# Top-32 attention with a gated feed-forward: weighted values of a head pair formed once per row group, and a longer lag from row 1920 on

## The chip, the cores and the metric

The kernel runs on one core of a Trainium2 chip. The metric is the time of one execution on the device in microseconds (us). TensorE is called PE here, its weight loads PEld, VectorE DVE, ScalarE ACT, GpSimd POOL and SyncE SP; SP issues all DMAs.

## The reference

Eight batches of eight heads attend over 576 rows with 64 channels a head. Of each row's 576 scores the 32 largest are kept, the softmax runs over these, and the result multiplies the values. The rows of all batches (8 x 576 = 4608, 512 channels each) then go through a gated feed-forward.

```python
scores = scale * np.matmul(q, k.transpose(0, 1, 3, 2))
kth = np.partition(scores, -top_k, axis=-1)[..., -top_k:-top_k + 1]
scores = np.where(scores >= kth, scores, -1000000000.0)
attn = np.exp(scores - np.max(scores, axis=-1, keepdims=True))
attn = attn / (np.sum(attn, axis=-1, keepdims=True) + 1e-09)
x = np.matmul(attn, v)             # then (4608, 512)
gate = 1.0 / (1.0 + np.exp(-(x @ w_gate)))
return gate * (x @ w_val) @ w_out  # d_ff = 1536
```

## The kernel before

**Tiling.** Attention works on one head pair of one row tile at a time (a step): 128 rows, or 64 for the fifth tile of a batch. Even batches are cut into the row groups tiles 0 to 2 and 3 to 4, odd ones into tiles 0 to 1 and 2 to 4; `steps` runs over row groups, then over the four head pairs, then over the tiles of the group. The feed-forward works on twelve units of 384 rows (`U`); a unit becomes available when the last row group that it needs is through for all four pairs.

**A step.** `scores` (L186) multiplies on PE and copies the scores from PSUM on ACT. `select` (L254) finds the 32nd largest with DVE, ACT and POOL, `masked` (L222) keeps what lies above it and forms in `inv` (L230) the reciprocal of the row sums. `turn` (L303) transposes the weights on PE into PSUM tiles `pt` (pool `ps_t`, two buffers), which ACT copies to the tile `et` (two buffers).

**The weighted values.** `weigh` (L322) is called for every two row tiles or for the rest of a group: 256, 128 or 64 columns. In blocks of 256 and 128 columns eight matmuls with 64-column weights (L330, L331) go in pairs, one head into the upper and one into the lower half of the PSUM tile `po` (pool `ps_o`, one buffer), and one matmul with 128-column weights (L332, `mixed`, the key chunk that both heads share) ends the sum. In the 64-column block there are eight with 64-column weights (L335, L336) and two with 64x64 weights (L337, L338). Each matmul on these plain f32 operands stands twice in the trace. Then `inv` is transposed into the same PSUM tile (L341), ACT copies it to `rs` (L344), DVE multiplies (L347 or L351), and ACT and POOL form the high and the low part of x (`xh`, `xl`; L354, L355).

**Order.** One program order is written out by `run`: attention steps, with the feed-forward's generators drawn in between. Through the first twenty-odd steps `split_weights` also splits the weights in high and low parts; when it is done, the pools `x` and `spare` are opened (`"spare" in pools`). From then on the feed-forward is drawn until its work reaches `goal = at - LAG`, where `at` is the number of attended rows and `LAG` is 448. A scheduler with its own timeline then sorts the instructions of each engine by priority, so matmuls of different parts come to stand between one another; each engine runs its own list strictly in that order.

The stretch of PE that the prediction speaks of is the whole list from about 250 us on. These lines decide when `weigh` is called:

```python
            if len(invs) == 2 or i >= end - 1 or i == NT - 1:
                ...
                weigh(et, values[g, p], o, invs, pieces, nm)
```

Of the kernel before, what the change touches and what calls it, by code (L numbers as in the profile page):

```python
# [10 lines left out]
F32 = mybir.dt.float32  # L11
# [5 lines left out]
AF = mybir.ActivationFunctionType  # L17
ALU = mybir.AluOpType
# [11 lines left out]
def tile_topk_attention_then_gated_ffn(  # L30
# [8 lines left out]
    nc = tc.nc  # L39
    P = 128  # L40
    B, H, _, S = k.shape
    D = P // 2
# [3 lines left out]
    REM = S - NT * P  # L46
# [9 lines left out]
    U = 3 * P  # L56
# [5 lines left out]
    FETCH, ASK, AHEAD = 2, 4, 2  # L62

    SOON, RUSH = 14, 22
    HELD = 2 * FG
    LAG = U + P // 2

    const = ctx.enter_context(tc.tile_pool(name="const", bufs=1))
    bi = ctx.enter_context(tc.tile_pool(name="bi", bufs=3))
# [3 lines left out]
    b1 = ctx.enter_context(tc.tile_pool(name="b1", bufs=1))  # L73
# [8 lines left out]
    ps_t = ctx.enter_context(tc.tile_pool(name="ps_t", bufs=2, space=bass.MemoryType.PSUM))  # L82
    ps_o = ctx.enter_context(tc.tile_pool(name="ps_o", bufs=1, space=bass.MemoryType.PSUM))
    ps_f = ctx.enter_context(tc.tile_pool(name="ps_f", bufs=3, space=bass.MemoryType.PSUM))

    ident = const.tile([P, P], F32, tag="ident", name="ident")
# [15 lines left out]
    pools, fresh, copies, ahead = {}, {}, [], []  # L102
# [119 lines left out]
    def masked(J, s, kth, st, e, nm):  # L222

        for j in range(J):
            nc.vector.scalar_tensor_tensor(  # L225
                e[:, j], s[:, j], kth[j], e[:, j], op0=ALU.is_ge, op1=ALU.mult, accum_out=st[:, 4 + j : 5 + j]
            )
        nc.gpsimd.tensor_scalar(st[:, 4 : 4 + J], st[:, 4 : 4 + J], 1e-9, None, op0=ALU.add)
        nc.vector.reciprocal(st[:, 6 : 6 + J], st[:, 4 : 4 + J])
        inv = bi.tile([P, P], F32, tag="inv", name=f"inv_{nm}")  # L230
        nc.gpsimd.tensor_copy(
            inv.rearrange("p (j d) -> p j d", j=J), st[:, 6 : 6 + J].unsqueeze(2).to_broadcast([P, J, P // J])
        )
        return e, inv
# [84 lines left out]
            nc.tensor.transpose(pt[:REM, 0], ef[:, NT * P : S], ident)  # L319
            nc.scalar.activation(et[:REM, 4, :P], pt[:REM, 0], AF.Copy)  # L320

    def weigh(et, vt, n, invs, pieces, nm):  # L322

        both = ps_o.tile([P, 4 * P], F32, tag="o", name=f"po_{nm}")
        po, rb = both[:, :n], both[:, 2 * P :]
        if n > REM:
            mixed = vt[:, 4:6].rearrange("p a d -> p (a d)")

            for c in reversed(range(4)):
                nc.tensor.matmul(po[D:], vt[:, 6 + c], et[:, 5 + c, :n], start=c == 3, stop=False)  # L330
                nc.tensor.matmul(po[:D], vt[:, c], et[:, c, :n], start=c == 3, stop=False)  # L331
            nc.tensor.matmul(po, mixed, et[:, 4, :n], start=False, stop=True)  # L332
        else:
            for c in range(4):
                nc.tensor.matmul(po[:D], vt[:, c], et[:, c, :REM], start=c == 0, stop=False)  # L335
                nc.tensor.matmul(po[D:], vt[:, 6 + c], et[:, c, REM:P], start=c == 0, stop=False)  # L336
            nc.tensor.matmul(po[:D], vt[:REM, 4], et[:REM, 4, :REM], start=False, stop=True)  # L337
            nc.tensor.matmul(po[D:], vt[:REM, 10], et[:REM, 4, REM:P], start=False, stop=True)  # L338

        for t, inv in enumerate(invs):  # L340
            nc.tensor.transpose(rb[:, t * P : (t + 1) * P], inv, ident)  # L341
        rs = b1.tile([P, 2 * P], F32, tag="rs", name=f"rs_{nm}")
        m = len(invs) * P
        nc.scalar.activation(rs[:, :m], rb[:, :m], AF.Copy)  # L344
        xf = rs[:, :n]
        if n > REM:
            nc.vector.tensor_tensor(xf, po, rs[:, :n], op=ALU.mult)  # L347
        else:
            for h in range(2):
                d = slice(h * D, h * D + D)  # L350
                nc.vector.tensor_tensor(xf[d], po[d], rs[d, h * REM : h * REM + REM], op=ALU.mult)  # L351
        o = 0
        for (xh, xl), c, k in pieces:
            nc.scalar.activation(xh[:, c : c + k], xf[:, o : o + k], AF.Copy)  # L354
            nc.gpsimd.tensor_tensor(xl[:, c : c + k], xf[:, o : o + k], xh[:, c : c + k], op=ALU.subtract)  # L355
            o += k
# [56 lines left out]
    def run(general):  # L413
        steps = [(g, p, i) for g, (_, first, end) in enumerate(groups) for p in range(NP) for i in range(first, end)]
        keys, values, qs, staged, xs = {}, {}, {}, {}, {}
# [34 lines left out]
            ffn_pools()  # L450
            splits = split_weights()
        todo, work, at, col, ready = [], 0, 0, 0, 0
        parts, done = {}, {}
        taken, steps_of = 0, ([2] * FG + [2, 0] * (NE // 2)) * NG

        for n in range(len(steps) + 2):
            if n < len(steps):
                g, p, i = steps[n]
                b, first, end = groups[g]
                m = n  # L460
                further = 1 if "spare" in pools else 0
                for m in range(fetched, n + FETCH + further + 1):
                    fetch(m)
                fetched = n + FETCH + further + 1
                get_values(n)
                for m in range(asked, n + ASK + further + 1):
                    ask(m)
                asked = n + ASK + further + 1
                for m in range(begun, n + AHEAD + further + 1):
                    begin(m)  # L470
                begun = n + AHEAD + further + 1
                J = 2 if i < NT else 1
                nm = f"{mark}{b}_{i}_{p}"
                if general:
                    parts[n] = select_any(J, staged.pop(n), nm)
                else:
                    parts[n] = select(J, staged.pop(n), col, nm)
                next(parts[n])
                col += J
            if n - 1 in parts:  # L480
                done[n - 1] = next(parts.pop(n - 1))
            if splits is not None:
                due = HELD * min(n + 1, SOON) // SOON
                if todo:
                    due = HELD + (2 * n_w - HELD) * (n + 1 - SOON) // (RUSH + 1 - SOON)
                while split < min(due, 2 * n_w):
                    while todo and taken < len(steps_of) and sum(steps_of[: taken + 1]) <= split:
                        work += next(todo[0])
                        taken += 1
                    next(splits)  # L490
                    split += 1
                if split == 2 * n_w:
                    while taken < len(steps_of):
                        work += next(todo[0])
                        taken += 1
                    next(splits, None)
                    splits = None
            else:
                goal = at - LAG
                goal *= 3 * (2 * NF * NP + NE * NF)  # L500
                while todo and work < goal:
                    cost = next(todo[0], None)
                    if cost is None:
                        todo.pop(0)
                    else:
                        work += cost
            if n < 2:
                continue
            g, p, i = steps[n - 2]
            b, first, end = groups[g]  # L510
            nm = f"{mark}{b}_{i}_{p}"
            e, inv = done.pop(n - 2)
            if i == first or (i - first) % 2 == 0 or i == NT:
                et, o, invs = b2.tile([P, 9, 2 * P], F32, tag="et", name=f"et_{nm}"), 0, []
            turn(e, i, et, o, nm)
            invs.append(inv)
            o += P if i < NT else REM
            if len(invs) == 2 or i >= end - 1 or i == NT - 1:

                t, left, pieces = b * S + (i + 1 - len(invs)) * P, o, []  # L520
                while left:
                    u = max(x for x, (t0, _) in enumerate(units) if t0 <= t)
                    c = t - units[u][0]
                    if (u, p) not in xs:
                        pool = bx if u % 3 < 2 else pools["x"]
                        xs[u, p] = [pool.tile([P, U], F32R, tag=x, name=f"{x}{mark}_{u}_{p}") for x in ("xh", "xl")]
                    cols = min(left, units[u][1] - c)
                    pieces.append((xs[u, p], c, cols))
                    t, left = t + cols, left - cols
                weigh(et, values[g, p], o, invs, pieces, nm)  # L530
            at += (P if i < NT else REM) / NP
            if p == NP - 1 and i == end - 1:
                while ready < len(units) and sum(units[ready]) <= b * S + min(end * P, S):
                    todo.append(ffn(f"{mark}{ready}", [xs[ready, d] for d in range(NP)], *units[ready]))
                    ready += 1
        for rest in todo:
            for _ in rest:
                pass

    run(False)  # L540


# [66 lines left out]
```

## Time and profile before

| what | value |
|---|---|
| median of the runs | 1595.59 us (1593.63, 1595.59, 1596.2) |
| the profiled execution, its own time | 1597.9 us |
| its span | 1596.1 us |
| PE busy, PEld busy | 96%, 88% |
| DVE, ACT, POOL busy | 82%, 72%, 67% |
| granted clock, mean | 0.979 of full speed |

A busy PE is not PE at its peak, since matmuls overlap: what one costs is read from the distance between the starts of two that follow each other, not from its duration. The span is cut by stretch in the windows, and the idle time of PE by its cause in the waits.

### The profile page before, as it was taken

The page shows a single profiled execution, that of the slowest core. Times are in us where ns is not written, and L with a number is a line of the kernel's source. Part 1 is how long each engine was busy: PE and PEld are TensorE (multiplying, and loading weights), DVE is VectorE, ACT ScalarE, POOL GpSimd, SP SyncE. Part 2 cuts the span into 40 slices and gives each one's busy share as a digit, 9 for nine tenths or more (in the row PEclk, how much of TensorE's full clock was granted, in tenths as well). Part 3 has the DMA queues.
Part 4 walks back from the last instruction along what each step waited for, and adds up shares of the span by engine and source line. Part 5 has one row for each costly group of instructions (what it writes and reads, how often), then busy time and mean ns, then how long its engine had stood idle before and what let it go on. Part 6 is the DMA issues. An engine that isn't in the chain of part 4 may idle for free.

```text
span 1596.1 us, 33487 instructions
## 1 busy us (share of the span) xinstructions
PE 1533.7 (96%) x10226; PEld 1403.4 (88%) x10226; DVE 1302.6 (82%) x5845; ACT 1144.5 (72%) x2547; POOL 1073.6 (67%) x1788
## 2 busy tenths in 40 slices
PE   5777999999999999999999999999999999999998
PEld 3555888789999999999999999999999999999998
DVE  7898899898988898888888889887988888877201
ACT  7788899887777777777777767767777777766221
POOL 6579765598767876777666976777667876665111
PEclk8678999999999999999999999999999999999999
DMA  7502576855555665565555665566555665564574
GB/s 241 177 27 79 180 234 234 281 185 204 190 201 209 208 235 191 205 236 204 190 201 199 223 234 190 208 225 214 191 201 199 219 220 193 192 207 168 180 283 160
DMA packets 87454, 319.99 MB, mean 200 GB/s; under 512 B 9696, under 2 KB 36320, under 8 KB 61920
## 3 DMA queue, kind: packets, MB, share of 16 engines
q1 hardware_dynamic: 87264, 317.76, 57.8%
q8 instruction: 83, 1.36, 0.3%
q14 instruction: 107, 0.88, 0.2%
HBM read 289.41 MB, written 28.31 MB: 199 GB/s over the span
## 4 chain that ended last, share of the span: by engine, by line
PE 84%; DVE 6%; ACT 4%; POOL 3%; DMA 2%; issue 2%; SPq 0%; ACTq 0%; POOLq 0%; DVEq 0%
PE pz L384 12%; PE pz L385 12%; PE pz L383 12%; PE pss L205 9%; PE pt L311 7%; PE po L330 6%; PE po L403 6%; PE po L402 6%; PE po L404 6%; PE po L332 2%; POOL u L289 2%; DMA wraw<-in_w_dram 1%; DVE cand L271 1%; PE po L341 1%; PE po L335 1%
## 5 line engine op out<-in xcount | busy, mean ns | idle before, releaser
L289 POOL TENSOR_TENSOR u<-s,under 128x288 f32<-128x288 f32 x576 | 449.1, 802 | 152.5 <-ACT under L283 143.3
L271 DVE MAX8 cand<-s 128x8 f32<-128x72 f32 x2304 | 348.2, 218 | 65.4 <-ACT s L212 63.5
L383 PE MATMUL pz<-xh,w 128*128 128x384 f32 x1056 | 362.0, 344 | 1.8 <-ACT gf L388 1.8
L384 PE MATMUL pz<-xl,w 128*128 128x384 f32 x1056 | 357.8, 339 | 0.0
L385 PE MATMUL pz<-xh,w 128*128 128x384 f32 x1056 | 357.5, 339 | 0.0
L225 DVE SCALAR_TENSOR_TENSOR e<-s,kths,e 128x576 f32<-128x576 f32 x288 | 269.6, 942 | 11.9 <-ACT e L220 10.1
L283 ACT ACTIVATE under<-s,leads 128x576 bf16<-128x576 f32 x288 | 222.6, 773 | 68.8 <-DVE leads L275 39.4
L299 DVE MAX8 kths<-u 128x8 f32<-128x584 f32 x288 | 218.7, 759 | 29.6 <-POOL u L290 28.2
L391 POOL TENSOR_TENSOR gl<-gf,gh 128x384 fp32r<-128x384 f32 x144 | 152.1, 1057 | 113.9 <-ACT gh L390 110.8
L205 PE MATMUL pss<-k,qh 128*128 128x288 f32 (+2 forms) x672 | 200.1, 315 | 22.8 <-ACT s L212 17.2
L312 ACT ACTIVATE et<-pt 128x384 f32<-128x384 f32 x384 | 179.2, 488 | 47.6 <-PE pt L311 47.0
L212 ACT ACTIVATE s<-pss 128x576 f32<-128x576 f32 x288 | 185.1, 643 | 39.0 <-PE pss L205 37.6
L220 ACT ACTIVATE e<-s,st 128x576 f32<-128x576 f32 x288 | 209.7, 773 | 2.8 <-POOL st L279 2.6
L383 PEld LDWEIGHTS pz<-xh,w 128*128 128x128 f32 x1056 | 198.5, 188 | 2.1 <-ACT gf L388 2.1
L384 PEld LDWEIGHTS pz<-xl,w 128*128 128x128 f32 x1056 | 198.7, 188 | 0.1
L385 PEld LDWEIGHTS pz<-xh,w 128*128 128x128 f32 x1056 | 198.4, 188 | 0.0
L311 PE MATMUL pt<-ident,e 128*128 128x128 f32 x1152 | 181.6, 279 | 14.8 <-DVE e L225 11.8
L205 PE MATMUL pss<-k,ql 128*128 128x288 f32 (+2 forms) x672 | 187.1, 300 | 0.0
L403 PE MATMUL po<-gl,w 128*128 128x384 f32 x528 | 179.3, 341 | 0.2 <-POOL gl L391 0.2
L404 PE MATMUL po<-gh,w 128*128 128x384 f32 x528 | 177.3, 339 | 0.0
L402 PE MATMUL po<-gh,w 128*128 128x384 f32 x528 | 175.7, 348 | 0.0
L311 PEld LDWEIGHTS pt<-ident,e 128*128 128x128 f32 x1152 | 144.1, 143 | 27.5 <-DVE e L225 9.5
(99 smaller groups left out, 3309.5 us busy)
## 6 DMA issues: line engine op xcount, KB each, us to landing
w<-ws SPq DMA_DIRECT2D x198, 1024.0 KB, 4.9
v<-in_v_dram SPq DMA_DIRECT2D x64, 352.0 KB, 3.4
qraw<-in_q_dram SPq DMA_DIRECT2D x160, 128.0 KB, 3.0
kraw<-in_k_dram SPq DMA_DIRECT2D x64, 288.0 KB, 3.3
wraw<-in_w_dram SPq DMA_DIRECT2D x36, 512.0 KB, 4.9
ws<-w_split SPq DMA_DIRECT2D x36, 512.0 KB, 4.7
out_dram<-acc SPq DMA_DIRECT2D x48, 192.0 KB, 5.7
```

The source lines that it names most:

```text
L205: nc.tensor.matmul(ps[:, half, o : o + n], x[:, h * P : (h + 1) * P], ks[h][:, k0 : k0 + n], start=t == 0, stop=t == len(todo) - 1,)
L225: nc.vector.scalar_tensor_tensor(e[:, j], s[:, j], kth[j], e[:, j], op0=ALU.is_ge, op1=ALU.mult, accum_out=st[:, 4 + j : 5 + j])
L271: nc.vector.max(cand[:, j, 8 * g : 8 * g + 8], s[:, j, g * SEG : (g + 1) * SEG])
L283: nc.scalar.activation(under[:, j], s[:, j], AF.Sign, bias=bound, scale=-CUT, accum_out=sums[:, j : j + 1])
L289: nc.gpsimd.tensor_tensor(u[:, j, part], s[:, j, part], under[:, j, part], op=ALU.mult)
L311: nc.tensor.transpose(pt[:, c], ef[:, k0 : k0 + P], ident)
L383: nc.tensor.matmul(ps, wt[:, u, 0, d], xh, start=d == 0, stop=False)
L384: nc.tensor.matmul(ps, wt[:, u, 0, d], xl, start=False, stop=False)
L385: nc.tensor.matmul(ps, wt[:, u, 1, d], xh, start=False, stop=d == NP - 1)
L402: nc.tensor.matmul(ps, wt[:, e % 2, 0, f], gh, start=f == 0, stop=False)
L403: nc.tensor.matmul(ps, wt[:, e % 2, 0, f], gl, start=False, stop=False)
L404: nc.tensor.matmul(ps, wt[:, e % 2, 1, f], gh, start=False, stop=f == FG - 1)
```

## The change

`weigh` now takes a list of blocks. As long as the weights are being split it is called as before; after that the blocks of a head pair are collected and it is called once at the end of each row group (`i == end - 1`). It takes the blocks from the last to the first. A last block of 128 columns begins with its `mixed` matmul (`early`), then come its 64-column matmuls, then those of the first block, and the first block's `mixed` ends. A last block of 64 columns comes first as a whole, its 64x64 matmuls at its end. `tc.issue_after` lets the second block's matmuls stand only behind the last one of the block before, and `RAISE` raises the priority of all of them. Where the product and the transposed reciprocals don't fit one PSUM tile (320 or 384 columns), the latter go to a tile `rb` of `ps_t`. `rs`, `xh` and `xl` are formed once for all blocks, with fewer and larger instructions on ACT and POOL; `inv` gets four buffers in `spare` and `rs` one of 384 columns. The lag grows from 448 to 512 rows between attended rows 1920 and 2688.

```diff
+    RAISE = 200
     LAG = U + P // 2
...
-        inv = bi.tile([P, P], F32, tag="inv", name=f"inv_{nm}")
+        inv = (pools["spare"] if "spare" in pools else bi).tile([P, P], F32, tag="inv", bufs=4 if "spare" in pools else 3, name=f"inv_{nm}")
...
-    def weigh(et, vt, n, invs, pieces, nm):
-        both = ps_o.tile([P, 4 * P], F32, tag="o", name=f"po_{nm}")
-        po, rb = both[:, :n], both[:, 2 * P :]
...
+    def weigh(blocks, vt, pieces, nm):
+        n = sum(cols for _, cols, _ in blocks)
+        m = sum(len(invs) for _, _, invs in blocks) * P
+        po = ps_o.tile([P, 4 * P], F32, tag="o", name=f"po_{nm}")
+        rb = po[:, 4 * P - m :]
+        if n + m > 4 * P:
+            rb = ps_t.tile([P, 4, P], F32, tag="t", name=f"rb_{nm}").rearrange("p a n -> p (a n)")[:, :m]
+        mixed = vt[:, 4:6].rearrange("p a d -> p (a d)")
+        at = [sum(cols for _, cols, _ in blocks[:x]) for x in range(len(blocks))]
+        last = None
+        for x in reversed(range(len(blocks))):
+            et, cols, _ = blocks[x]
+            top = po[:, at[x] : at[x] + cols]
+            early = x > 0 and cols > REM
+            with ExitStack() as queued:
+                queued.enter_context(tc.high_priority(offset=RAISE))
+                if early:
+                    nc.tensor.matmul(top, mixed, et[:, 4, :cols], start=True, stop=False)
+                if last is not None:
+                    queued.enter_context(tc.issue_after(last.ins))
+                if cols > REM:
+                    for c in reversed(range(4)):
+                        for d, v0, e0 in ((slice(D, P), 6, 5), (slice(0, D), 0, 0)):
+                            last = nc.tensor.matmul(
+                                top[d],
+                                vt[:, v0 + c],
+                                et[:, e0 + c, :cols],
+                                start=c == 3 and not early,
+                                stop=c == 0 and early,
+                            )
+                else:
...
+                if cols > REM and not early:
+                    nc.tensor.matmul(top, mixed, et[:, 4, :cols], start=False, stop=True)
+        for t, inv in enumerate(inv for _, _, invs in blocks for inv in invs):
+            nc.tensor.transpose(rb[:, t * P : (t + 1) * P], inv, ident)
...
-        nc.scalar.activation(rs[:, :m], rb[:, :m], AF.Copy)
+        nc.scalar.activation(rs[:, :m], rb, AF.Copy)
...
-                goal = at - LAG
+                goal = at - LAG - P // 2 * min(max(at - 5 * U, 0) / (2 * U), 1)
...
-                t, left, pieces = b * S + (i + 1 - len(invs)) * P, o, []
+                if not blocks:
+                    base = b * S + (i + 1 - len(invs)) * P
+                blocks.append((et, o, invs))
+            if blocks and (i == end - 1 or "spare" not in pools):
+                t, left, pieces = base, sum(cols for _, cols, _ in blocks), []
...
-                weigh(et, values[g, p], o, invs, pieces, nm)
+                weigh(blocks, values[g, p], pieces, nm)
+                blocks = []
```


PE, batch 2, head pair 1, its first row group (tiles 0 to 2; `po_b_i_p` and `pt_b_i_p` are the PSUM tiles of batch, tile and pair, `pss` scores, `pz` and `po2` the feed-forward). Before:

```order
L404 MATMUL po2_2_0_1_6880<-gh_2_0_1_6453,w_2_12_6758 128x384
L330 MATMUL po_2_1_1_6636<-et_2_0_1_6486,v_4_1_6344 64x256
...
L332 MATMUL po_2_1_1_6636<-et_2_0_1_6486,v_4_1_6344 128x256
L341 MATMUL po_2_1_1_6636<-ident_105,inv_2_0_1_6263 128x128
...
L205 MATMUL pss_2_1_3_0_6660<-k_4_3_6_6504,ql_2_1_3_6349 128x288
L330 MATMUL po_2_2_1_6791<-et_2_2_1_6775,v_4_1_6344 64x128
...
L332 MATMUL po_2_2_1_6791<-et_2_2_1_6775,v_4_1_6344 128x128
L341 MATMUL po_2_2_1_6791<-ident_105,inv_2_2_1_6582 128x128
```

The same place now:

```order
L312 MATMUL pt_2_2_1_2_6747<-ident_105,e_2_2_1_6349 128x128 x2
L341 MATMUL po_2_2_1_6754<-et_2_2_1_6736,v_4_1_6324 128x128
L312 MATMUL pt_2_2_1_2_6747<-ident_105,e_2_2_1_6349 128x128
L364 MATMUL rb_2_2_1_6755<-ident_105,inv_2_0_1_6228 128x128
...
L410 MATMUL pz_2_1_0_0_6992<-xl_2_3_4310,w_2_4_6988 128x384
L347 MATMUL po_2_2_1_6754<-et_2_2_1_6736,v_4_1_6324 64x128 x8
L347 MATMUL po_2_2_1_6754<-et_2_0_1_6466,v_4_1_6324 64x256 x8
L361 MATMUL po_2_2_1_6754<-et_2_0_1_6466,v_4_1_6324 128x256
L206 MATMUL pss_2_1_3_1_6627<-k_4_3_7_6490,qh_2_1_3_6328 128x288
```

The two runs of 64-column matmuls, of 256 and of 128 columns, became one; the 128-column block's mixed matmul and the transpositions moved ahead of it, and the `mixed` of the first block ends it.

PE, batch 3, head pair 1, second row group (tiles 2 to 4: a block of 256 columns and one of 64). Before:

```order
L383 MATMUL pz_4_1_1_0_10854<-xh_4_0_7816,w_4_5_10850 128x384
L330 MATMUL po_3_3_1_10630<-et_3_2_1_10482,v_7_1_10392 64x256
...
L332 MATMUL po_3_3_1_10630<-et_3_2_1_10482,v_7_1_10392 128x256
L341 MATMUL po_3_3_1_10630<-ident_105,inv_3_2_1_10327 128x128
...
L383 MATMUL pz_4_1_1_1_10867<-xh_4_3_8634,w_4_5_10850 128x384
L335 MATMUL po_3_4_1_10777<-et_3_4_1_10767,v_7_1_10392 64x64
...
L337 MATMUL po_3_4_1_10777<-et_3_4_1_10767,v_7_1_10392 64x64
L338 MATMUL po_3_4_1_10777<-et_3_4_1_10767,v_7_1_10392 64x64
L341 MATMUL po_3_4_1_10777<-ident_105,inv_3_4_1_10564 128x128
```

The same place now:

```order
L410 MATMUL pz_4_1_1_1_10903<-xl_4_3_8731,w_4_5_10886 128x384
L356 MATMUL po_3_4_1_10669<-et_3_4_1_10659,v_7_1_10336 64x64
L357 MATMUL po_3_4_1_10669<-et_3_4_1_10659,v_7_1_10336 64x64
...
L358 MATMUL po_3_4_1_10669<-et_3_4_1_10659,v_7_1_10336 64x64
L359 MATMUL po_3_4_1_10669<-et_3_4_1_10659,v_7_1_10336 64x64
L347 MATMUL po_3_4_1_10669<-et_3_2_1_10426,v_7_1_10336 64x256 x8
L361 MATMUL po_3_4_1_10669<-et_3_2_1_10426,v_7_1_10336 128x256
L206 MATMUL pss_3_3_3_1_10570<-k_6_3_7_8870,qh_3_3_3_10340 128x288
```

The 64-column block moved in front of the 256-column one: 64-column, 64x64 and again 64-column matmuls follow each other with nothing in between, and the block's transposition no longer stands behind its 64x64 matmuls.

PE, batch 6, head pair 0, second row group (tiles 3 and 4). Before:

```order
L402 MATMUL po2_8_2_1_19413<-gh_8_2_2_19143,w_8_16_19300 128x384
L330 MATMUL po_6_3_0_19194<-et_6_3_0_19176,v_13_0_18916 64x128
...
L332 MATMUL po_6_3_0_19194<-et_6_3_0_19176,v_13_0_18916 128x128
L341 MATMUL po_6_3_0_19194<-ident_105,inv_6_3_0_18969 128x128
...
L404 MATMUL po2_8_2_1_19413<-gh_8_2_3_19267,w_8_16_19300 128x384
L335 MATMUL po_6_4_0_19327<-et_6_4_0_19317,v_13_0_18916 64x64
...
L337 MATMUL po_6_4_0_19327<-et_6_4_0_19317,v_13_0_18916 64x64
L338 MATMUL po_6_4_0_19327<-et_6_4_0_19317,v_13_0_18916 64x64
L341 MATMUL po_6_4_0_19327<-ident_105,inv_6_4_0_19139 128x128
```

The same place now:

```order
L410 MATMUL pz_8_2_3_1_19320<-xl_8_3_15448,w_8_11_19303 128x384
L356 MATMUL po_6_4_0_19088<-et_6_4_0_19076,v_13_0_18670 64x64
...
L312 MATMUL pt_6_3_1_0_19221<-ident_105,e_6_3_1_18846 128x128 x3
...
L206 MATMUL pss_6_4_2_0_18830<-k_12_2_5_17186,ql_6_4_2_18553 128x64
L358 MATMUL po_6_4_0_19088<-et_6_4_0_19076,v_13_0_18670 64x64
L359 MATMUL po_6_4_0_19088<-et_6_4_0_19076,v_13_0_18670 64x64
L347 MATMUL po_6_4_0_19088<-et_6_3_0_18935,v_13_0_18670 64x128 x8
L361 MATMUL po_6_4_0_19088<-et_6_3_0_18935,v_13_0_18670 128x128
L364 MATMUL po_6_4_0_19088<-ident_105,inv_6_3_0_18723 128x128
```

The eight 64-column matmuls of the 64-column block stand by themselves as before, with transpositions, feed-forward and scores behind them; its 64x64 matmuls moved in front of the 128-column block.

## Rows read from the trace of the kernel before

**Rows 1.** The page's head: span, and busy time, share and instructions of each engine.

```profile
span 1596.1 us, 33487 instructions
PE 1533.7 (96%) x10226; PEld 1403.4 (88%) x10226; DVE 1302.6 (82%) x5845; ACT 1144.5 (72%) x2547; POOL 1073.6 (67%) x1788
```

**Rows 2.** Windows: stretch, length, busy us by engine (instructions), then clock, DMA, GB/s.

```profile
400.00:600.00 200.00, 200.00 (x1432) 188.16 (x1432) 175.72 (x824) 148.66 (x336) 149.70 (x250) 1.00 0.60 206
...
1500.00:1550.00 50.00, 50.00 (x306) 49.09 (x305) 7.40 (x16) 11.04 (x25) 8.47 (x10) 1.00 0.70 250
```

**Rows 3.** Waits of PE from 185 to 400 us: total, times, longest.

```profile
PE pz L383 <- ACT gf L388: 1.8, 1, 1.8
PE pz L385 <- ACT w_split L149: 1.4, 1, 1.4
...
PE po L403 <- POOL gl L391: 0.2, 1, 0.2
```

**Rows 4.** Timeline of PE at 416 us (start, duration, line, tiles, shapes): one 256-column block.

```profile
416.13 0.34 PE L385 MATMUL pz<-xh,w 128*128 128x384 f32 x1
416.31 0.34 PE L383 MATMUL pz<-xh,w 128*128 128x384 f32 x1
416.58 0.43 PE L330 MATMUL po<-et,v 128*64 128x256 f32 x1
...
416.84 0.38 PE L330 MATMUL po<-et,v 128*64 128x256 f32 x1
...
417.06 0.38 PE L330 MATMUL po<-et,v 128*64 128x256 f32 x1
...
418.14 0.38 PE L330 MATMUL po<-et,v 128*64 128x256 f32 x1
...
418.45 0.70 PE L332 MATMUL po<-et,v 128*128 128x256 f32 x2
418.99 0.38 PE L341 MATMUL po<-ident,inv 128*128 128x128 f32 x2
```

**Rows 5.** Timeline of PE at 267 us: a mixed matmul behind full-size ones.

```profile
266.98 0.59 PE L332 MATMUL po<-et,v 128*128 128x256 f32 x2
267.41 0.38 PE L341 MATMUL po<-ident,inv 128*128 128x128 f32 x2
```

**Rows 6.** Timeline of PE at 400 us: a run of 64-column matmuls cut off by scores.

```profile
400.35 0.22 PE L335 MATMUL po<-et,v 128*64 128x64 f32 x1
...
400.41 0.22 PE L335 MATMUL po<-et,v 128*64 128x64 f32 x1
...
400.57 0.40 PE L205 MATMUL pss<-k,qh 128*128 128x288 f32 x1
400.81 0.29 PE L205 MATMUL pss<-k,ql 128*128 128x288 f32 x1
400.94 0.30 PE L205 MATMUL pss<-k,qh 128*128 128x288 f32 x1
```

**Rows 7.** Timeline of PE at 709 us: the end of a 64-column block.

```profile
709.68 0.22 PE L335 MATMUL po<-et,v 128*64 128x64 f32 x1
...
709.84 0.27 PE L337 MATMUL po<-et,v 64*64 64x64 f32 x1
...
709.94 0.22 PE L337 MATMUL po<-et,v 64*64 64x64 f32 x1
...
710.10 0.33 PE L341 MATMUL po<-ident,inv 128*128 128x128 f32 x1
710.18 0.38 PE L205 MATMUL pss<-k,ql 128*128 128x288 f32 x1
```

**Rows 8.** Waits of ACT, whole span, and the page's group of `et` copies.

```profile
ACT et L312 <- PE pt L311: 47.0, 65, 2.8
ACT under L283 <- POOL u L289: 17.6, 20, 2.6
...
L312 ACT ACTIVATE et<-pt 128x384 f32<-128x384 f32 x384 | 179.2, 488 | 47.6 <-PE pt L311 47.0
```

More of the change, by code (lines that the diff above doesn't have):

```diff
@@ L320, in turn @@
             nc.scalar.activation(et[:REM, 4, :P], pt[:REM, 0], AF.Copy)
-    def weigh(et, vt, n, invs, pieces, nm):
-        both = ps_o.tile([P, 4 * P], F32, tag="o", name=f"po_{nm}")
-        po, rb = both[:, :n], both[:, 2 * P :]
[L326 to L332, printed above, removed]
-        else:
[L334 to L343, printed above, removed]
-        nc.scalar.activation(rs[:, :m], rb[:, :m], AF.Copy)
-        xf = rs[:, :n]
[L346 to L351, printed above, removed]
@@ new lines, in weigh @@
+    def weigh(blocks, vt, pieces, nm):
[29 more added lines that the diff above has]
+                else:
+                    for c in range(4):
+                        nc.tensor.matmul(top[:D], vt[:, c], et[:, c, :REM], start=c == 0, stop=False)
+                        nc.tensor.matmul(top[D:], vt[:, 6 + c], et[:, c, REM:P], start=c == 0, stop=False)
+                    nc.tensor.matmul(top[:D], vt[:REM, 4], et[:REM, 4, :REM], start=False, stop=True)
+                    last = nc.tensor.matmul(top[D:], vt[:REM, 10], et[:REM, 4, REM:P], start=False, stop=True)
+                if cols > REM and not early:
+                    nc.tensor.matmul(top, mixed, et[:, 4, :cols], start=False, stop=True)
+        for t, inv in enumerate(inv for _, _, invs in blocks for inv in invs):
+            nc.tensor.transpose(rb[:, t * P : (t + 1) * P], inv, ident)
+        if "spare" in pools:
+            rs = pools["spare"].tile([P, 3 * P], F32, tag="rs", name=f"rs_{nm}")
+        else:
+            rs = b1.tile([P, 2 * P], F32, tag="rs", name=f"rs_{nm}")
+        nc.scalar.activation(rs[:, :m], rb, AF.Copy)
+        xf = rs[:, :n]
+        for (_, cols, _), o in zip(blocks, at):
+            if cols > REM:
+                nc.vector.tensor_tensor(xf[:, o : o + cols], po[:, o : o + cols], rs[:, o : o + cols], op=ALU.mult)
+            else:
+                for h in range(2):
+                    d, r = slice(h * D, h * D + D), o + h * REM
+                    nc.vector.tensor_tensor(xf[d, o : o + cols], po[d, o : o + cols], rs[d, r : r + cols], op=ALU.mult)
@@ L452, in run @@
         todo, work, at, col, ready = [], 0, 0, 0, 0
-        parts, done = {}, {}
+        parts, done, blocks = {}, {}, []
         taken, steps_of = 0, ([2] * FG + [2, 0] * (NE // 2)) * NG
```

## The prediction

> **What bounds the kernel now.** I read the page's head, the windows, the waits of PE and then PE's timeline, in that order. The head gives the span, 1596.1 us, and PE busy for 96% of it, DVE for 82%, ACT for 72%, POOL for 67% [rows 1]. Busy PE alone would not make it the bound, since matmuls overlap. The windows say more: from 400 us on PE has no idle time at all, at full granted clock (1.00, the level of 2.4 GHz), while DVE stands at 176 of 200 us; late in the kernel the other engines are nearly empty and PE is full [rows 2]. The waits agree: from 185 to 400 us six of them hold PE for 5.0 us in all, from 1.8 down to 0.2 us [rows 3]; from 400 us on the list is empty. So from there the time is the sum of the distances at which PE's matmuls start, and an edit counts only by what it does to these, or by a wait that it brings.
>
> A feed-forward matmul follows the one before it after 0.18 us (416.13 to 416.31) [rows 4]. The distances are longer in one place: where PE goes from full-size weights to 64-column ones, between these and 64x64 ones, and back. I call each such change a switch and price it by the rows:
> - In, from full-size to 64-column: the last full-size matmul takes 0.27 instead of 0.18, and the first pair of narrow ones 0.26 instead of 0.22 (416.31, 416.58, 416.84, 417.06) [rows 4]. At the resolution of the rows 0.13, over many such places 0.14 us; I take **0.14**.
> - Between 64-column and 64x64: the last pair takes 0.16 where its like takes 0.06 [rows 6, 7], the first 64x64 pair 0.10; if that one would cost 0.05 in a stream, which is half its distance, the switch costs **0.15**.
> - Out, to a mixed matmul: the last pair takes 0.31 instead of 0.22, the two passes of the mixed matmul 0.54 (418.14, 418.45, 418.99) [rows 4] where they take 0.43 behind full-size matmuls [rows 5]. That is **0.20**. Out to scores: the last pair 0.16 instead of 0.06, the first score matmul 0.24 where the next takes 0.13 [rows 6], again 0.20; I take that for the feed-forward too.
> - Out to a transposition: the last pair 0.16, of which 0.10 is the switch, and the transposition 0.08, of which I count 0.06: **0.16** [rows 7].
>
> **The change part by part.** It removes no matmul: counted in both programs, PE has the same matmuls of the same shapes, and 160 transpositions of `inv` in either. What it removes is 40 ACT copies to `rs`, 40 ACT copies to `xh` and 40 POOL subtractions to `xl`, because 40 pairs of calls became 40 single ones. That lies beside a PE that never waits, on engines with a quarter or more of their time free [rows 1, 2]: 0 us. It would count only if PE had waits to shorten; the 5.0 us before 400 us are all there are.
>
> What it moves is PE's order, and there the switches can be counted one by one. Up to about 255 us both orders are the same. From there on the counts are, before and after: in 99 and 85; between 28 and 41; out to a transposition 27 and 12; out to anything else 72 and 73. By the prices that is
> before 99 x 0.14 + 28 x 0.15 + 27 x 0.16 + 72 x 0.20 = 36.8 us,
> after 85 x 0.14 + 41 x 0.15 + 12 x 0.16 + 73 x 0.20 = 34.6 us,
> so **-2.2 us**. It is this little because the order does not keep the runs whole. A three-tile group that stays whole, as batch 2 pair 1 in the order, saves one way in and one out, 0.34 us; a group with a 64-column block that stays whole, as batch 3 pair 1, saves about 0.15; split, as batch 6 pair 0, it saves nothing. Of the 28 groups with a 64-column block 18 are split, four of the twelve three-tile groups are cut by scores, and in the groups of two tiles, which the edit does not touch, two more cuts appear (15 ways in before, 17 after).
>
> The one price that no row shows is the switch from 64x64 back to 64-column, which stands 28 times in the new order and never in the old. Its lower bound is 0: then the sum is -2.2 - 28 x 0.15 = -6.4 us. Its upper bound is a way out and a way in, 0.34: then it is -2.2 + 28 x 0.19 = +3.1 us. I take 0.15, that of the same switch in the other direction, its nearest row. The Trainium skill ("TensorEngine Tiling (Array Packing)", Key Properties) says that each change of tiling mode, not of the tile alone, drains the engine; the rows of the other switches agree, and by that page the lower bound falls away and the sum stays at -2.2 us.
>
> The new `weigh` brings three waits into question. Its first block is read last, so of the two `et` tiles one is held until the end of the run, and ACT, which would copy the next pair's weights there, would have the copies of scores and of the feed-forward queued behind it. `rb` takes one of the two `ps_t` tiles in 28 groups, and the transpositions of the next tile stand behind it on PE. `inv` is held until the group's end, and on POOL the products for the next selection queue behind a blocked `inv`; it has four buffers in place of three. In the new order at least some 3.7 us of PE work lie between the end of `rb` and the second next user of that pool, 1.8 us between a transposition and the first matmul that needs its copy (1.9 before), and a copy takes 0.49 us, ACT having waited for the transpositions 65 times, for 47.0 us [rows 8]. I cost them at 0 and keep the loss for the rivals.
>
> The lag moves 64 of 4608 rows of feed-forward behind attention: 64/384 of a unit's 432 matmuls, 72 x 0.18 = 13 us of PE work, from one stretch in which PE is full to another in which it is full [rows 2]. In both orders the last scores stand ahead of the last unit's first matmul. 0 us either way.
>
> Between 255 and 400 us the order changes most: 18 transpositions and one 256-column block of weighted values that stood ahead of the last weight split now stand behind it. The waits there, 5.0 us [rows 3], can go, or come again in other places. I take no difference, with 5 us to either side.
>
> **Sum.** -2.2 us on the profiled execution's 1597.9 us (span 1596.1, 1.8 around it) is 1595.7. That execution lies 2.3 us above the median of the runs, 1595.59, by which the kernel is measured; on the median the forecast is 1593.4 us. About 0.2%, 3.2 us, is what can be told from no change here: below 1592.4 is faster, above 1598.8 slower.
>
> **The rivals.**
> (1) The way back from 64x64 costs nothing: -6.4 us, 1589.2. For it: both use the same 64-column half of the array; against it: the other direction costs 0.15.
> (2) The waits after the split go: -2.2 less 3 to 5, 1588.4 to 1590.4. For it: the split ends with less in front of it. Against: DVE is the fullest of the others, and its selection work is only moved.
> (3) The same waits double: -2.2 plus 3 to 5, 1596.4 to 1598.4; half a step more attention now stands between the split and the second unit.
> (4) Slower: the run comes up on PE before its copies are there. ACT stood for up to 2.6 us behind a product of POOL [rows 8]; with the copy's 0.49 that is 3.1 us after the transposition. In 13 places the new order leaves less than that between transposition and reader (5 in the old), and what they lack adds up to 6.7 us: 1600.1 us. It decides from the point where ACT runs behind PE by more than about 2 us at these places. Against it: the 5 places of before lack 4.1 us by the same count and show no wait, and ACT waited 65 times for a transposition, not PE for it.
> That the groups are scattered by the order, so that the edit does not do what it says, is inside the forecast by its counts.
>
> **How the numbers follow.** Forecast, PE stays the bound and the switches are priced as above, 1593.4 give or take 1.5: 0.52, of which 0.12 lies below 1592.4. Rival 1: 0.10, faster. Rival 2: 0.15, faster. Rival 3: 0.13, of which 0.03 is slower. Rival 4: 0.10, slower. So faster 0.37, within 0.2% 0.50, slower 0.13. The range runs from just below rival 2's gain to rival 4: 1588.0 to 1600.0 us; what lies outside is rival 1 together with rival 2, half of rival 4, and waits that no row of before hints at.
>
> **What would show it.** In the trace after: PE without waits from 400 us on, and its busy time still that of the span; the distance from the last 64x64 pair to the second 64-column pair, 0.15 above a stream's if the forecast holds, 0 for rival 1; the waits of PE from 185 to 400 us near 5 us, near 0 for rival 2, near 10 for rival 3; for rival 4 waits of the 64-column matmuls for ACT's `et`, or of transpositions for `rs`. ACT and POOL should be less busy by the removed copies without the time moving by that. The forecast is wrong if a wait of PE appears after 400 us, or if the distances of the matmuls outside the switches differ.

## The result: slower by 0.8 per cent, made in one stretch

The changed kernel takes 1608.2 us (median of six runs, 1606.5 to 1609.8), the kernel before beside it 1596.4: ratio 1.0076, 95% interval 1.0063 to 1.0089, so 10 to 14 us more. 1593.4 was forecast, with a range of 1588.0 to 1600.0. It was wrong in sign and by more than the range allowed.

The head of the page after answers to [rows 1], the two long stretches to [rows 2]; columns as there.

```profile
span 1608.0 us, 33179 instructions
PE 1538.1 (96%) x10226; PEld 1409.2 (88%) x10226; DVE 1307.3 (81%) x5845; ACT 1134.1 (71%) x2467; POOL 1077.6 (67%) x1748
...
PEclk8788999989999999999999999999999999999999
```

```profile
400.00:600.00 200.00, 200.00 (x1437) 190.12 (x1437) 169.65 (x776) 143.09 (x310) 137.11 (x231) 1.00 0.60 210
1500.00:1550.00 50.00, 50.00 (x307) 47.67 (x306) 7.40 (x16) 9.82 (x21) 8.98 (x9) 1.00 0.66 235
```

From 400 us on PE still has nothing but full stretches, at full granted clock (the share of its full clock that the chip allows TensorE), and PE's share of the span is as before: these lines don't show where the loss is. They show only one thing that is new, an 8 among the PEclk digits behind the start, in the slice from 322 to 362 us. There the rows differ: the last stretch of the weight split and two behind it, in the kernel before and then in the changed kernel (stretch, length, busy of PE, PEld, DVE, ACT, POOL, granted clock, then DMA):

```profile
285.00:300.00 15.00, 13.61 (x77) 12.09 (x76) 14.97 (x54) 14.05 (x30) 8.71 (x12) 1.00 0.79 266
...
310.00:330.00 20.00, 19.57 (x140) 15.70 (x140) 16.18 (x96) 15.96 (x36) 14.58 (x28) 1.00 0.53 176
330.00:350.00 20.00, 17.83 (x122) 16.65 (x122) 18.74 (x77) 15.74 (x38) 19.31 (x28) 1.00 0.67 230
```

```profile
285.00:300.00 15.00, 15.00 (x77) 12.74 (x76) 10.11 (x37) 9.07 (x18) 3.72 (x7) 1.00 0.94 322
...
310.00:330.00 20.00, 15.90 (x108) 12.05 (x106) 19.02 (x95) 16.59 (x39) 18.95 (x33) 1.00 0.46 146
330.00:350.00 20.00, 15.48 (x90) 12.83 (x91) 18.67 (x89) 14.60 (x34) 18.99 (x31) 0.74 0.40 127
```

From 285 to 300 us DVE is now busy for 10 of 15 us in place of all 15, and ACT and POOL for less; from 310 to 350 us DVE and POOL are nearly full and PE is the one that stands: 31.4 busy us in 40 in place of 37.4. Attention was held up before the split ended and is caught up afterwards, and meanwhile PE has too little to do. The waits of PE from 185 to 400 us, which answer to [rows 3], come to 11.6 us in place of 5.0 (total, times, longest):

```profile
PE pt L312 <- DVE e L226: 2.6, 3, 1.6
PE pt L312 <- ACT et L313: 2.5, 3, 1.9
PE pz L410 <- POOL xl L381: 2.5, 2, 1.3
PE pss L206 <- ACT s L213: 2.0, 3, 1.0
PE pz L411 <- ACT w_split L150: 1.4, 2, 1.1
...
```

Unit 1's last matmul, found by counting the matmuls of the built order against PE's records, starts at 450.4 us; in the kernel before at 440.0. So 10.4 of the 12 us are there by then. From there to the last unit's last matmul it is 1151.7 us in place of 1150.2.

**Where attention stopped.** POOL's rows of `inv` (start, duration, line, tiles; in the bracket the idle time ahead and what ended it), kernel before, then kernel after:

```profile
255.37 0.61 POOL L231 COPY inv<-st 128x128 f32<-128x128 f32 x1 [0.78 <-DVE st L229]
...
268.96 0.74 POOL L231 COPY inv<-st 128x128 f32<-128x128 f32 x1
...
278.85 0.54 POOL L231 COPY inv<-st 128x128 f32<-128x128 f32 x1 [1.64 <-DVE st L229]
```

```profile
293.12 0.77 POOL L232 COPY inv<-st 128x128 f32<-128x128 f32 x3
293.97 0.52 POOL L280 TENSOR_SCALAR st<-tops 128x2 f32<-128x2 f32 x2
```

Before, one `inv` every ten to sixteen us; after, none between 224 and 293 us and then three at once, with two new sets of statistics `st` directly behind them. And the exponentials on ACT, which need `st`, before and after:

```profile
253.33 1.44 ACT L220 ACTIVATE e<-s,st 128x576 f32<-128x576 f32 x2
...
263.29 1.45 ACT L220 ACTIVATE e<-s,st 128x576 f32<-128x576 f32 x2
...
276.95 1.45 ACT L220 ACTIVATE e<-s,st 128x576 f32<-128x576 f32 x2 [0.76 <-POOL st L279]
...
290.62 1.48 ACT L220 ACTIVATE e<-s,st 128x576 f32<-128x576 f32 x2
```

```profile
252.28 1.44 ACT L221 ACTIVATE e<-s,st 128x576 f32<-128x576 f32 x2 [2.54 <-POOL st L280]
...
300.17 4.09 ACT L221 ACTIVATE e<-s,st 128x576 f32<-128x576 f32 x6
```

After 253.7 us no exponential runs for 46 us, and then three tiles' worth in a row. The reason that I read from this, and that the runs below test: from the end of the split in program order, `inv` comes from the pool `spare`. That pool is laid over memory of the split, and in the built program the four buffers of `inv` have addresses within the raw tile that holds the first half of the last weight block. On the chip the split is then still going on; DVE's last read of that tile in the changed kernel ends at 290.0 us:

```profile
289.33 0.68 DVE L145 SCALAR_TENSOR_TENSOR wt_frac<-wraw 128x512 fp32r<-128x512 uint32 x1
```

`inv` reads `st`, of which there are three (pool `bi`): three tiles of statistics wait for three `inv`, and the next tile has none to write to. No row shows POOL waiting for the raw tile itself: the scheduler has put `inv` late in POOL's list, behind two other products (`gl` from 290.05 us, `ql` from 292.05 us), so that the dependence is seen only beside the kernel before.

### The profile page after: what moved, and what is told of

Its sections match the earlier page's. It is cut to its first block, busy times and chain, and to the rows that moved or that the text cites. A ratio compares the mean times of both kernels' runs of the same rounds, so it can differ in the third digit from the quotient of the medians.

```text
span 1608.0 us, 33179 instructions
## 1 busy us (share of the span) xinstructions
PE 1538.1 (96%) x10226; PEld 1409.2 (88%) x10226; DVE 1307.3 (81%) x5845; ACT 1134.1 (71%) x2467; POOL 1077.6 (67%) x1748
## 4 chain that ended last, share of the span: by engine, by line
PE 80%; DVE 8%; POOL 4%; ACT 3%; issue 2%; DMA 2%; SPq 0%; POOLq 0%; ACTq 0%; DVEq 0%
PE pz L410 12%; PE pz L411 12%; PE pz L409 12%; PE pss L206 9%; PE po L347 6%; PE pt L312 6%; PE po L428 6%; PE po L429 6%; PE po L430 6%; POOL u L290 2%; DVE cand L272 2%; PE po L361 2%; DVE e L226 2%; DMA wraw<-in_w_dram 2%; PE po L356 1%
## 5 line engine op out<-in xcount | busy, mean ns | idle before, releaser
L226 DVE SCALAR_TENSOR_TENSOR e<-s,kths,e 128x576 f32<-128x576 f32 x288 | 283.9, 991 | 2.3 <-ACT e L221 1.8
```

What stands on the lines that cost most here:

```text
L226: nc.vector.scalar_tensor_tensor(e[:, j], s[:, j], kth[j], e[:, j], op0=ALU.is_ge, op1=ALU.mult, accum_out=st[:, 4 + j : 5 + j])
```

## The experiments

Theory 1: the loss comes from a tile whose new place is memory that the split still reads (first I took `rs`). Theory 2: joined weighing gives unit 1 and 2 their rows too late. Theory 3: the loss is a sum of small ones, switches and waits, all along the kernel. Ratios are to the kernel before on the same chip.

**rs_place** and **inv_place**, each one new place alone in the kernel before:

```diff
-        rs = b1.tile([P, 2 * P], F32, tag="rs", name=f"rs_{nm}")
+        if "spare" in pools:
+            rs = pools["spare"].tile([P, 3 * P], F32, tag="rs", name=f"rs_{nm}")
+        else:
+            rs = b1.tile([P, 2 * P], F32, tag="rs", name=f"rs_{nm}")
```

> The kernel before with one line changed: from the end of the weight split on, the scaling tile rs is taken from the pool that is laid over the memory of the split's own tiles, as in the changed kernel; weighing, its order of writing, inv and the lag stay as before. Theory 1 (the place of rs): the first rs after the split must wait for the last weight split to give its memory back, with it the one output tile of the weighing and everything behind it; ACT's exponentials gather behind the split, and attention has to be caught up while PE waits between 310 and 345 us: 1604 to 1609 us, with PE idle in that stretch, the granted clock there falling, and unit 1's last matmul near 450 us instead of 440. Theory 2 (the joined weighing gives a unit's rows too late): nothing is joined here, so 1595 to 1598 us. Theory 3 (the loss is a sum of many small ones after 450 us): 1595 to 1599 us.

```diff
-        inv = bi.tile([P, P], F32, tag="inv", name=f"inv_{nm}")
+        inv = (pools["spare"] if "spare" in pools else bi).tile([P, P], F32, tag="inv", bufs=4 if "spare" in pools else 3, name=f"inv_{nm}")
```

> The kernel before with only the tile inv taken, from the end of the split on, from the pool over the split's memory (four buffers in place of three); rs, weighing and lag as before. Theory 1: inv is needed earlier than rs, but lies over raw weights that are read earlier than the last ones; the order changes from 267 us on instead of 255: a part of the loss, 1597 to 1605 us, less than for rs. Theories 2 and 3: 1595 to 1598 us.

`rs` alone: 1.0015 (1.0005 to 1.0024), 1 to 4 us. `inv` alone: 1.0109 (1.0094 to 1.0123), 15 to 20 us, more than the whole change. So it is a place, but that of `inv`; my first guess of the tile was wrong. (In the built program `rs` lies over the same raw tile, but its first copy there is due only behind the split: at 305.6 us in the kernel before, at 301.8 in rs_place.) The rows of inv_place are like those of the changed kernel, POOL and ACT:

```profile
292.53 1.42 POOL L231 COPY inv<-st 128x128 f32<-128x128 f32 x3
```

```profile
250.09 1.45 ACT L220 ACTIVATE e<-s,st 128x576 f32<-128x576 f32 x2
...
299.96 4.10 ACT L220 ACTIVATE e<-s,st 128x576 f32<-128x576 f32 x6
```

**joined_from_365**: the changed kernel, with joining and both places beginning at step 34.

```diff
+            if n == 34:
+                pools["late"] = pools["spare"]
+            late = "late" in pools
...
-            if blocks and (i == end - 1 or "spare" not in pools):
+            if blocks and (i == end - 1 or not late):
...
-        inv = (pools["spare"] if "spare" in pools else bi).tile([P, P], F32, tag="inv", bufs=4 if "spare" in pools else 3, name=f"inv_{nm}")
+        inv = (pools["late"] if "late" in pools else bi).tile([P, P], F32, tag="inv", bufs=4 if "late" in pools else 3, name=f"inv_{nm}")
```

(`rs` and the raised priority by the same flag.)

> The changed kernel, but joined weighing and the new places of rs and inv begin at step 34 of 160 (on PE at 365 us) and not at the end of the split; before that everything is as in the kernel before, and from unit 3 on the order on PE is that of the changed kernel. Theory 1: the loss was made before 365 us, so it goes: 1596 to 1599 us (the changed kernel lost another 1.4 us between unit 1's end and its own end). Theory 2: the later groups are joined all the same, and only unit 1's are not; if it is unit 1 alone that comes late, this kernel gives 1596 to 1599 too, but then the run with nothing joined must be back there as well. Theory 3: the loss stays, 1605 to 1609 us.

1.0004 (0.9994 to 1.0014): the loss is gone, though from unit 3 on PE's order is that of the changed kernel. Theory 3 falls.

**nothing_joined**: each block weighed as it comes, all else as changed.

```diff
-            if blocks and (i == end - 1 or "spare" not in pools):
+            if blocks:
```

> The changed kernel with the joining undone: each block of one or two tiles is weighed by itself as soon as it is there, as in the kernel before; raised priority, places of rs and inv and the lag stay as changed. Theory 1: the loss stays, 1605 to 1610 us, with PE waiting between 310 and 345 us. Theory 2: the loss goes, 1595 to 1598 us. Theory 3: the part of it that lies in the joined runs goes, 1596 to 1602 us.

1.0094 (1.0078 to 1.0109): the loss stays without joining, with 10.8 us of PE's waits from 185 to 400 us. Theory 2 falls.

**inv_back**: the changed kernel with `inv` from its old pool.

```diff
-        inv = (pools["spare"] if "spare" in pools else bi).tile([P, P], F32, tag="inv", bufs=4 if "spare" in pools else 3, name=f"inv_{nm}")
+        inv = bi.tile([P, P], F32, tag="inv", name=f"inv_{nm}")
```

> The changed kernel with inv taken throughout from its old pool of three buffers; the place of rs, joined weighing, raised priority and lag as changed. The first runs gave 1613 us for the kernel before with only inv moved, 1598.8 with only rs moved. Theory 1, now with inv for rs (inv lies over the raw weights of the last split, POOL writes it only when these are read, three sets of statistics st are held meanwhile and ACT's exponentials stand still from 254 to 300 us): the loss goes, and 1595 to 1600 us are left, with exponentials at 263 and 277 us as in the kernel before. Theory 1 as first told (rs): the loss stays, 1605 to 1609 us.

1.0020 (1.0011 to 1.0029): most of the loss goes. What stays, 2 to 5 us, is about what `rs`'s place (1 to 4) gives by itself. It isn't lost in this stretch, since unit 1's last matmul starts at 438.8 us, before the 440.0 of the kernel before; what makes it is not shown.

**more_st_before, more_st_inv_place, more_st_after**: by which way does a late `inv` hold attention up? It holds three `st`, and it holds the weighing, whose one output tile and two `et` hold the transpositions. Eight buffers of `st` take away the first way and leave the second. In both `select` functions:

```diff
-        st = bi.tile([P, 8], F32, tag="st", name=f"st_{nm}")
+        st = bi.tile([P, 8], F32, tag="st", bufs=8, name=f"st_{nm}")
```

> The kernel before with eight buffers in place of three for the small tile of statistics st; nothing else. The partner of the next run: what these buffers do by themselves. The scheduler's order changes from 127 us on, with more switches (in 110, between 28, out to a transposition 28, out to anything else 82: by the prices 40.5 us, 3.7 more than before). Both theories: 1596 to 1601 us.

> The kernel of the run inv_place (inv over the split's memory, 1613 us) with eight buffers of st in place of three. inv is still written only at the end of the split, near 293 us; but the statistics of three tiles no longer hold up the next ones. Theory 1 by way of st (POOL's blocked inv holds st, and without st no exponential starts): exponentials go on at 263 and 277 us and the loss of 16 us goes but for some 2 to 4 us: 1596 to 1601 us, near its partner. Theory 1 by another way (the weighing that waits for inv holds its output tile and the et tiles, and these hold everything): the loss stays, 1608 to 1614 us.

> The changed kernel with eight buffers of st in place of three; places of inv and rs, joined weighing, priority and lag as changed. Switches by the order 32.6 us, 4.2 less than before. Theory 1 by way of st: the loss of the stretch at 310 to 345 us goes but for 2 to 4 us; with the waits for acc of the new lag, some 2 us, 1595 to 1600 us. Theory 1 by way of the output tile: 1604 to 1609 us.

By themselves the buffers cost something: 1.0033 (1.0021 to 1.0045), 3 to 7 us, where the switches of the new order say 3.7. With them `inv`'s place costs nothing more: 0.9998 (0.9989 to 1.0008) in place of 1.0109. That is even less than the 1.0033 of the buffers alone; the place changes the order too, and this gain was not taken apart. And the changed kernel comes to 1.0027 (1.0016 to 1.0039) in place of 1.0076, no slower than the kernel before with the same buffers. The rows of more_st_inv_place decide it, POOL and then ACT:

```profile
303.47 1.00 POOL L231 COPY inv<-st 128x128 f32<-128x128 f32 x4
```

```profile
268.37 1.43 ACT L220 ACTIVATE e<-s,st 128x576 f32<-128x576 f32 x2
...
282.02 1.44 ACT L220 ACTIVATE e<-s,st 128x576 f32<-128x576 f32 x2
...
296.17 1.45 ACT L220 ACTIVATE e<-s,st 128x576 f32<-128x576 f32 x2 [0.38 <-POOL st L279]
```

`inv` is now ten us later still, four in a row, and the exponentials run through. So the late weighing by itself does no such harm; the held statistics did it.

**old_lag, raised_more, not_raised**: the rest of the change, without the fault. All three are joined_from_365 with the old lag, and differ in the priority of the weighing's matmuls (200, 1000, 0).

```diff
-    RAISE = 200
+    RAISE = 1000
...
-                goal = at - LAG - P // 2 * min(max(at - 5 * U, 0) / (2 * U), 1)
+                goal = at - LAG
```

> The run joined_from_365 with the lag of the kernel before to the end. By the order on PE the switches between kinds of matmuls are, before and here: in 99 and 74, between 28 and 17, from 64x64 back to 64-column 0 and 27, out to a transposition 27 and 10, out to anything else 72 and 64. With the prices of the prediction (0.14, 0.15, 0.15, 0.16, 0.20) that is 36.8 and 31.4: 5.4 us less than before, 1591.5 us, and 3.2 less than joined_from_365. If the lag costs nothing beyond its switches, that is the difference. Rival: the waits at the ends of units 5 and 10 in the changed kernel, some 5 us, come from the lag: then up to 1589. Rival: the switches are not what the time after 365 us is made of: 1596 to 1598, no difference from joined_from_365.

> The run old_lag with the priority of the weighing's matmuls raised by 1000 in place of 200, so that fewer runs are cut: in 66, between 18, back 27, out to a transposition 11, out to anything else 55, by the prices 28.8 us, 8.0 less than before and 2.6 less than old_lag. Theory of the prices: 1589 us. Rival: the raised matmuls come up before their copies are there and PE waits for ACT's et: as slow as old_lag or slower, 1592 to 1598, with waits of PE after 365 us.

> The run old_lag with the priority raised by 0: the joined runs are there, but the scheduler cuts them: in 119, between 21, back 26, out to a transposition 50, out to anything else 69, by the prices 45.5 us, 8.7 more than before. Theory of the prices: 1605 us. Rival: joining itself is what pays or costs, whatever the cuts: as old_lag within 2 us.

Up to 365 us these four kernels have the order of the kernel before. Switches by the orders and the prices of the prediction, PE's waits after 400 us from the waits view, their sum, and the time measured, all as differences to the kernel before in us:

| kernel | switches | waits | sum | measured (95%) | ratio |
|---|---|---|---|---|---|
| joined_from_365 | -2.2 | 2.3 | 0.1 | 0.6 (-1.0 to 2.2) | 1.0004 |
| old_lag | -5.4 | 1.9 | -3.5 | -3.7 (-5.3 to -2.1) | 0.9977 |
| raised_more | -8.0 | 1.4 | -6.6 | -7.3 (-9.4 to -5.1) | 0.9954 |
| not_raised | 8.7 | 0.0 | 8.7 | 10.5 (8.0 to 12.9) | 1.0066 |

The sums lie inside all four intervals; the waits in them were read afterwards and not forecast. The prices hold, and raised_more, 1589.97 us, is faster than both kernels.

**more_st_raised**: the changed kernel with eight `st`, the old lag and priority 1000, joined from the end of the split on.

```diff
-    RAISE = 200
+    RAISE = 1000
...
+        st = bi.tile([P, 8], F32, tag="st", bufs=8, name=f"st_{nm}")
...
+                goal = at - LAG
```

> The run more_st_after with the lag of the kernel before and the priority raised by 1000: the whole change with the two faults mended in place, without a later start of the joining. Switches by the order 28.8 us, 8.0 less than before. Theory 1 by way of st with the prices: 2 to 4 us above the run raised_more (1590 us), so 1590 to 1594 us. If the stretch at the end of the split still costs what it did in the changed kernel: 1600 us or more.

0.9984 (0.9975 to 0.9993), 1593.1 us: within what was expected, faster than both kernels as well, and by the ratios 5 us behind raised_more, which leaves the end of the split alone.

Where the order changes before 400 us as well, the sum is looser. With PE's waits from 185 us on taken in it gives 5.6 us for more_st_before, measured 5.3, and -2.2 for more_st_raised, measured -2.6, but 2.2 for more_st_after, measured 4.3 (2.6 to 6.2).

## Why the prediction was wrong, point by point

- **PE is the bound after 400 us.** Right in the main, but not wholly without waits, and a wait there was a sign that the prediction itself had named against it. Three rows, four waits, 2.3 us:

```profile
PE po L428 <- ACT acc L432: 1.1, 2, 0.7
PE po L428 <- DVE acc L434: 0.7, 1, 0.7
PE pss L206 <- ACT s L213: 0.5, 1, 0.5
```

  None of them is one that the prediction named: mostly the feed-forward's output matmuls wait for a sum `acc` to free their PSUM tile. They are as long as the gain of the switches, which by the table is why joined_from_365 is no faster than the kernel before.

- **The prices of the switches.** Right, the one that no row had shown included. A whole run in the changed kernel at 789 us, 64x64 between two widths of 64-column matmuls:

```profile
789.52 0.22 PE L356 MATMUL po<-et,v 128*64 128x64 f32 x1
789.53 0.22 PE L357 MATMUL po<-et,v 128*64 128x64 f32 x1
789.68 0.27 PE L358 MATMUL po<-et,v 64*64 64x64 f32 x1
789.69 0.27 PE L359 MATMUL po<-et,v 64*64 64x64 f32 x1
789.79 0.22 PE L358 MATMUL po<-et,v 64*64 64x64 f32 x1
789.80 0.22 PE L359 MATMUL po<-et,v 64*64 64x64 f32 x1
789.95 1.95 PE L347 MATMUL po<-et,v 128*64 128x256 f32 x16
791.82 0.70 PE L361 MATMUL po<-et,v 128*128 128x256 f32 x2
```

  The last 64x64 pair takes 0.16 (789.79 to 789.95) where a like pair takes 0.06: 0.10. The eight 256-column pairs take 1.87 to the mixed matmul; take off 0.31 for the last, as on the way out, and six of 0.216 (0.22 in the rows), and the first has taken 0.26: some 0.05 more. With all digits, from the last 64x64 pair to the second 256-column pair it is 0.422 in the median of the 14 places after 400 us, where 0.057 + 0.216 would be a stream's: 0.149 for the way back, 0.15 forecast. Rival 1, that it is free, falls.

- **The copies removed cost nothing.** Nothing speaks against it: ACT's and POOL's shares moved by a per cent or none, and no wait of PE followed them.

- **The three waits of the new `weigh`.** Here `inv` was seen and costed at 0, and the step failed. The prediction asked how long a buffer of `inv` is held, found four in place of three, and let it be. It did not ask when the first of the four could be written at all. That stood in the diff: `inv` moves to a pool that is laid over the split's memory. Nor did it ask what a late `inv` keeps: three `st`, and through them every exponential.

- **The lag, "0 us either way".** Wrong as a price, though its effect lay inside the counts. With it the order has 85 ways in, without it 74 (old_lag against joined_from_365): 3.2 us by the prices, 4.3 measured (0.9977 against 1.0004, whose intervals do not meet).

- **"Between 255 and 400 us ... I take no difference, with 5 us to either side."** The failed term: +10.4 us. The prediction saw that 18 transpositions and a weighing had moved behind the last split and took it for a scheduler's choice, neutral on the whole. It was the trace of a dependence. Counted in the built programs, 227 transpositions stand ahead of the last split's matmuls in the kernel before and 209 in the changed kernel; the same 209 stand in inv_place and nothing_joined, which lose in the same stretch, and 224 or 227 in every other run. So the sign of it was there before the run. Waits went from 5.0 to 11.6 us: somewhat more than rival 3's total, but not its waits, since the longest of before, for `gf`, is gone, and those for `et` and `xl`, 2.5 us each, are new. And there was a second part that no rival had, the clock. While PE was waiting, its granted clock fell. Four short windows after:

```profile
332.50:335.00 2.50, 0.60 (x4) 0.31 (x3) 2.50 (x17) 2.50 (x6) 2.34 (x4) 0.84 0.00 0
335.00:337.50 2.50, 2.33 (x9) 2.33 (x10) 2.01 (x18) 1.82 (x6) 2.25 (x5) 0.50 0.63 170
...
342.50:345.00 2.50, 2.50 (x27) 1.95 (x25) 2.50 (x15) 1.94 (x4) 2.44 (x6) 0.62 0.74 239
345.00:347.50 2.50, 2.50 (x23) 1.59 (x21) 2.50 (x16) 2.37 (x5) 2.26 (x6) 1.00 0.66 237
```

  0.50 is the level of 1.2 GHz. From about 334 to 344 us PE ran at it, and was busy for some 8 us of that (2.33, 1.56 and 2.23 in the three windows from 335 to 342.5, and about 1.9 of the next). Full clock would have saved somewhat under half of it: a feed-forward matmul follows the one before after 0.32 us there in place of 0.18 (rows in the last section), so 3.5 to 4 us. With 6.6 us more waits that makes 10 to 10.6, against 10.4 measured. That sum is an estimate; no run separated the two parts.

- **Rivals 2 and 4.** The waits did not go. The run did not come up before its copies: no 64-column matmul of the changed kernel waits for `et` after 400 us (one in old_lag, 0.8 us).

The mechanism that was forecast, fewer switches, is real, and measured in four kernels. The sign came from the place of one tile, `inv`, and from the few `st` that it held.

## What to carry to other kernels

When a tile moves to a pool that lies over another stage's memory, ask three things: when on the chip (not in program order) that memory is last read, which instruction then waits, and what that instruction keeps while it waits. Here eight buffers in place of three, of a tile of 32 bytes per partition, took away 8 of the changed kernel's 12 us (1.0076 to 1.0027) and all of inv_place's 17. And where an order is scheduled and PE is the bound, count the switches in the built order: a change that makes runs longer is worth as much as the runs that stay uncut, so check that the scheduler leaves them whole.

## What was not expected of the hardware

PE's granted clock fell to the lower level in the middle of the kernel. Ahead of it PE had been busy for 8.17 us of 310 to 320 us, 3.72 of 320 to 325, 4.01 of 325 to 330, 1.26 of 330 to 332.5 and 0.60 of the 2.5 us in the window in which it fell. It was back at 1.00 from 345 us on, after the busy windows above. At the lower level a feed-forward matmul follows the one before after 0.32 us, not 0.18 [rows 4]:

```profile
340.75 0.52 PE L411 MATMUL pz<-xh,w 128*128 128x384 f32 x1
341.07 0.52 PE L410 MATMUL pz<-xl,w 128*128 128x384 f32 x1
341.39 0.52 PE L411 MATMUL pz<-xh,w 128*128 128x384 f32 x1
```

The kernel before was idle in one such window too (0.66 us busy of 332.5 to 335) and kept 1.00. What tells the two apart is not shown. That it had been busy for 19.57 of the 20 us from 310 to 330 does not explain it: joined_from_365, old_lag and raised_more have its order on PE there and within 0.1 us its waits from 310 to 350 us, and in the profiled execution of each the clock fell as well, at about 335 us, and was back by 340. The kernel before, then raised_more:

```profile
332.50:335.00 2.50, 0.66 (x6) 0.39 (x4) 2.33 (x20) 2.50 (x7) 2.33 (x5) 1.00 0.94 383
```

```profile
332.50:335.00 2.50, 0.95 (x3) 0.95 (x4) 2.30 (x17) 2.50 (x7) 2.33 (x5) 0.85 0.96 395
335.00:337.50 2.50, 2.50 (x9) 2.50 (x9) 1.35 (x10) 0.96 (x3) 2.42 (x5) 0.50 0.58 169
```

What sets the changed kernel, inv_place and nothing_joined apart is how long the lower level lasted in this stretch: about 10 us or more, in one piece or in two. So a stall of PE can cost more than its length, and that belongs in the bound of any wait.
